# Gate and up weight gradients from one 512-column product, gate_w's gradient as one row, sines in one batch, the narrow products inside z

## The chip, the cores and the metric

The kernel runs on one core of a Trainium2 chip. The metric is the device time of one execution in microseconds (us). Five engines work side by side, each through its own queue in order: TensorE (PE in the profile; PEld are its weight loads), VectorE (DVE), ScalarE (ACT), GpSimd (POOL) and SyncE (SP), which here only issues DMAs. A matmul takes a stationary operand of up to 128 x 128 and streams the columns of a moving operand past it; its result goes to PSUM, from which ScalarE or VectorE copies it out ("evacuates" it) so that the PSUM buffer can be used again.

## The reference

The forward function mixes a spectral filter with a gated feed-forward network; the kernel computes its output and all gradients for a given `grad_out`. S = 2048 tokens, D = 576, F = 4608, all bf16.

```python
g = sigmoid((x * gate_w).sum(-1, keepdims=True))
a = irfft2(rfft2(x) * (w_r + 1j * w_i))                 # over tokens and features
b = (gelu(x @ w_gate) * (x @ w_up)) @ w_down
out = g * a + (1 - g) * b
# returned: out and the gradients of x, w_r, w_i, w_gate, w_up, w_down, gate_w
```

With da, the gradient at the hidden layer, the kernel needs A = gelu(.)*up, and the gradients dHg and dHu of the two hidden products; then dW_gate = x^T dHg, dW_up = x^T dHu and dW_down = A^T (grad_out (1 - g)).

## The kernel before

**First stage (up to 977 us).** The hidden width is cut into NG = 18 groups of FG = 256 columns. Each group takes four *steps* m = 0..3, one for each 512 tokens (four tiles of 128 tokens), so there are 72 steps `pr` = 4g + m. A step does on TensorE: 16 full matmuls of `z` (grad_out x w_down^T, L402, 256 columns) and 4 with 64 contraction rows (L407), 4 such ones of `xy` (L411, 512 columns: gate and up side by side), and two halves of 8 full ones (L418). ScalarE then reads z into `da` (L430) and each half of xy into `xb`, `hu` and `q` (L439, L440, L437). VectorE prepares the gelu (`H_ew1`, L445 to L447), ScalarE takes two sigmoids (L461, L462), and eight VectorE operations (`H_ew2`, L466 to L473) make A, dHu and dHg, which are kept in SBUF and also stored to a scratch tensor (L477).

**Weight gradients.** While group g runs, TensorE also does the products of group g - 1, which `W_units` hands out in portions to the four steps: `u_dwd` (dW_down: 4 units of 16 matmuls of 288 columns, L508), `u_dw` (dW_gate and dW_up over 512 of the 576 features: four units, each two PSUM halves of 16 matmuls with 256 columns, L527), and `tail` (the last 64 features: 16 pairs of matmuls with 64 stationary columns, L544). All share the PSUM pool `wps` of two buffers. A finished unit is evacuated by `wevac` (L486), on ScalarE as a rule, on VectorE while `wcopy[0]` says so, and stored from GpSimd's queue (L534, L518, L548).

**The spectral part.** Its 2-D transforms are a list of some 200 units of 2 to 12 matmuls (L574, L591, L683, L772, L818 and others). `want(pr)` says how many have to be done by step pr; `FIRST` lists this for the first eight steps. The first unit of a step goes between the matmuls of the second half of xy, the others between the portions of weight-gradient work ("jobs"), evenly by the jobs' estimated weights. All these units share a single PSUM buffer, which is also that of z: a unit can't begin before ScalarE has evacuated the one before it, and z of the next step not before the step's last one is out. An evacuation stands in ScalarE's queue where its unit was issued: that of the first unit before the reading of the second half of xy, that of the second one behind it.

**Tables.** The transforms need tables of sines. `build_R` and `build_B` compute angles on VectorE and put the sine itself on a list; `run_late` issues the listed sines on ScalarE (L170, L238), at steps 5 and 7. ScalarE needs another activation table for a sine than for a sigmoid. At steps 4 and 5, `scale_dB` multiplies grad_out by (1 - g), 16 tiles of 128 x 576, half on ScalarE (L956), half on VectorE (L958).

In group 0 the steps also hold the transposes of x and grad_out (`titems`, through two PSUM buffers `pg`) and the gate (`gate`, L383 to L387), which makes g.

**Second stage (from 977 us).** Every matmul has 288 columns (L1159): the output b, and the gradient of x. It ends with `x_last` for the last token tile. `gate_grad`, just before it, sums the gate's gradient over tokens by 10 matmuls (L1210) into a column of 576 numbers spread over the partitions, which GpSimd's queue stores by two DMAs with 2-byte elements (L1216, L1217). The last two stores of the x gradient are issued by SP (L1242).

```python
return [[d[0]], [d[1], d[2], d[3]], [tl_, w[0]], [w[1], w[2]], w[3]]   # L555: jobs of m = 0, 1, 2, 3; w[3] is carried to the next m = 0
FIRST = (0, 0, 0, 0, 0, 0, 3, 5)                                       # L921
tables = {5: 4, 7: 1}.get(pr)                                          # L1045: run_late before this job
```

Of the kernel before, what the change touches and what calls it, by code (L numbers as in the profile page):

```python
# [30 lines left out]
FG = 256  # L31
# [213 lines left out]
def kernel(  # L245
# [212 lines left out]
    def H_ew2(g, m, tiles, s, da):  # L458
        xb, q, hu = tiles
        om = ewt("om", g)  # L460
        nc.scalar.activation(om[:], s[:], ACT.Sigmoid, scale=-2.0 * C_GELU)  # L461
        nc.scalar.activation(s[:], s[:], ACT.Sigmoid, scale=2.0 * C_GELU)  # L462
        A = keepA.tile([P, 4, FG], BF16, tag="A", name="A")
        dHg = keep.tile([P, 4, FG], BF16, tag="dHg", name="dHg")
        dHu = keep.tile([P, 4, FG], BF16, tag="dHu", name="dHu")
        V.tensor_tensor(xb[:], xb[:], s[:], op=ALU.mult)  # L466
        V.tensor_tensor(q[:], xb[:], q[:], op=ALU.mult)
        V.tensor_tensor(om[:], om[:], q[:], op=ALU.mult)
        V.tensor_tensor(A[:], xb[:], hu[:], op=ALU.mult)
        V.tensor_tensor(dHu[:], da[:], xb[:], op=ALU.mult)  # L470
        V.tensor_tensor(om[:], om[:], s[:], op=ALU.add)
        V.tensor_tensor(hu[:], da[:], hu[:], op=ALU.mult)
        V.tensor_tensor(dHg[:], hu[:], om[:], op=ALU.mult)  # L473
        fsl = slice(g * FG, (g + 1) * FG)
        def store():
            for k, tl in enumerate((A, dHg, dHu)):
                LD.dma_start(scr[k][m][:, :, fsl].rearrange("t p f -> p t f"), tl[:])  # L477
        stores.append(store)
        kept.setdefault(g, []).append((A, dHg, dHu))
# [8 lines left out]
    def W_units(g):  # L488
# [3 lines left out]
        def tl(k, t):  # L492
            return kt[t // 4][k][:, t % 4, :]
# [27 lines left out]
        def u_dw(k, ov, c0, cut=T // 2):  # L521
            both = cut != T // 2

            def f(cc, t0, t1):
                wps = wtile(("w", k, c0))
                for t in range(t0, t1):
                    nc.tensor.matmul(wps[:, cc, :], lhsT=xn[:, t, (c0 + cc) * P:(c0 + cc + 1) * P],  # L527
                                     rhs=tl(k, t), start=(t == 0 and (cc == 0 or not both)),
                                     stop=(t == T - 1 and (cc == 1 or not both)))
                if cc == 0 or t1 < T:  # L530
                    return
                dw = stage.tile([P, TPB, FG], BF16, tag="dw", name="dw")
                wevac(dw[:], wps[:])
                wst[0].dma_start(ov[:, c0:c0 + TPB, fsl], dw[:])  # L534
            parts = [(cc, t0, t1) for cc in range(TPB) for t0, t1 in ((0, cut), (cut, T))]
            if both:
                parts.sort(key=lambda a: a[1])
            return [(1.7 * (a[2] - a[1]) / T, lambda a=a: f(*a)) for a in parts]
# [11 lines left out]
        tl_ = [(2.0, tail)]  # L550
        w = [u_dw(k, ov, c0, 12 if g == 0 and k == 1 else T // 2) for k, ov in ((1, o4v), (2, o5v)) for c0 in range(0, 4, TPB)]
        d = [u_dwd(fch, h) for fch in range(FCH) for h in range(2)]
        if g == 0:
            return [[w[0][:2], w[1][:2]], [w[0][2:], w[1][2:], tl_, d[0]], d[1:], [w[2]], w[3]]
        return [[d[0]], [d[1], d[2], d[3]], [tl_, w[0]], [w[1], w[2]], w[3]]  # L555
# [365 lines left out]
    FIRST = (0, 0, 0, 0, 0, 0, 3, 5)  # L921
# [31 lines left out]
    def scale_dB(n, on_act=False):  # L953
        for t in range(scaled[0], min(scaled[0] + n, T)):
            if on_act:
                nc.scalar.activation(dB[:, t, :], dB[:, t, :], ACT.Copy, scale=omg32[:, t:t + 1])  # L956
            else:
                V.tensor_scalar(dB[:, t, :], dB[:, t, :], omg32[:, t:t + 1], None, op0=ALU.mult)  # L958
            scaled[0] = t + 1

    for g in range(NG):
# [3 lines left out]
        for m in range(NPR):  # L965
# [3 lines left out]
            hs = [h for u in pend[m] for h in u] if pend else []  # L969

# [9 lines left out]
            if g == 0:  # L980
                def items(src, dst, t, *cp):
                    return titems(src, dst, 4 * t, (pgtile,) * 3, cp)
                head_, early, mid_, late_ = [
                    ([opening], [], items(dB, dOT, 1, VC, VC, VC) + items(xn, xT, 1, VC, VC, VC)
                     + [lambda: build_R(nc, tb, unit, 4)] + items(dB, dOT, 2, AC, AC, VC), []),
                    ([], items(xn, xT, 2, VC, VC, VC), [], items(dB, dOT, 3, AC, AC, VC)),
                    ([], items(xn, xT, 3, VC, VC, VC), [], []),
                    ([], [], [], [])][m]
                if m == 1:
                    rest.append(late_.pop())  # L990
                elif m == 2:
                    head_ = [rest.pop()]
                z, xy_full = H_mm(g, m, head_)
                da = H_da(g, m, z)
                for f in early:
                    f()
                if held:
                    held.pop()()
                xy = xy_full(0)
                for f in mid_:  # L1000
                    f()
                if m == 0:
                    columns_B(nc, tb, res)
                elif m == 1:
                    next(makeB)
                for part in (1, 0):
                    H_act(0, xy, tiles, part)
                xy = xy_full(1)
                for part in range(2):
                    H_act(1, xy, tiles, part)  # L1010
# [5 lines left out]
                for f in late_:  # L1016
                    f()
                state += [H_ew1(g, tiles), da]
                held.append(sigs)
            else:  # L1020
                z, xy_full = H_mm(g, m)
# [6 lines left out]
                xy = xy_full(1, fft_next if n else None)  # L1028
# [3 lines left out]
                if pr == 4:  # L1032
                    scale_dB(8, True)
                elif pr == 5:
                    scale_dB(8)
                elif pr == 6:
                    build_R(nc, tb, unit, 8)
                    next(makeB)
                elif pr == 7:
                    build_R(nc, tb, unit, 12)  # L1040
# [3 lines left out]
                at, k = 0.0, min(n, 1)  # L1044
                tables = {5: 4, 7: 1}.get(pr)  # L1045
# [64 lines left out]
    for _, h in carry + [h for us in pend[:4] for u in us for h in u] + pend[4]:  # L1110
        h()
    ps1.close()
# [10 lines left out]
    with tc.tile_pool(name="p2f", bufs=4, **kw) as p2f, \  # L1123
# [81 lines left out]
        def gate_grad():  # L1205
            gps = pacc.tile([P, 512], F32, tag="acc", name="gps")
            for c in range(5):
                n = min(P, D - c * P)
                for v in range(2):
                    nc.tensor.matmul(gps[0:n, c:c + 1], lhsT=gsplit[:, v, c * P:c * P + n], rhs=ones[:],  # L1210
                                     start=(v == 0), stop=(v == 1))
            dgw = p2s.tile([P, 5], BF16, tag="dgw", name="dgw")
            V.tensor_copy(dgw[:, 0:4], gps[:, 0:4])
            V.tensor_copy(dgw[LO, 4:5], gps[LO, 4:5])
            with nc.allow_non_contiguous_dma(reason="one column of 576 numbers"):
                ST.dma_start(out_7[0:512].rearrange("(c p) -> p c", p=P), dgw[:, 0:4])  # L1216
                ST.dma_start(out_7[512:D].rearrange("(p o) -> p o", o=1), dgw[LO, 4:5])  # L1217
# [96 lines left out]
```

## Time and profile before

| What | Value |
|---|---|
| Time, median of 3 runs | 1411.79 us (1410.51 to 1412.84) |
| The profiled execution's own time | 1411.65 us |
| Its span, first to last instruction | 1409.9 us |
| Mean granted TensorE clock | 0.996 |
| First stage / second stage | 0 to 977 us / 977 to 1409.9 us |
| VectorE, ScalarE busy over the span | 731.1 us, 738.6 us (52% each) |
| GpSimd busy | 225.4 us (16%) |
| DMA traffic | 214.62 MB, mean 152 GB/s |

A matmul's busy time overlaps that of its neighbours, so TensorE's busy share isn't how close it comes to its peak; the distance between the starts of matmuls is read from the timeline instead: n matmuls in a row that together last L, one of which lasts l, start (L - l)/(n - 1) apart. In the lists of waits each line gives who waited for whom, the total in us, how often, and the longest.

### The profile page before, as it was taken

How to read it: one execution, taken by the hardware profiler on the slowest of the kernel's cores; microseconds unless marked ns; L12 is line 12 of the kernel's file. 1: busy time of each engine (PE TensorE's matmuls, PEld its weight loads, DVE VectorE, ACT ScalarE, POOL GpSimd, SP SyncE). 2: the span in 40 equal slices, each digit the busy share in tenths (PEclk: the TensorE clock that was granted, in tenths of full speed). 3: DMA queues.
4: the chain of work that ended last, by engine and by line, in shares of the span. 5: the costliest groups of instructions: out<-in, count | busy, mean ns of one | idle time of the engine just before them, and what ended most of it. 6: DMA issues, size and time to landing. Idle time of an engine off the chain costs nothing.

```text
span 1409.9 us, 28154 instructions
## 1 busy us (share of the span) xinstructions
PE 1387.4 (98%) x11430; PEld 1027.5 (73%) x11430; DVE 731.1 (52%) x1393; ACT 738.6 (52%) x1334; POOL 225.4 (16%) x420
## 2 busy tenths in 40 slices
PE   8989999999999999999999999999999999999997
PEld 6566767676667766776776767778777777777776
DVE  7776565655788787785566565560001742122100
ACT  6877676777888888767777776661000000000000
POOL 3010100112343643322010100110000110000000
PEclk9999999999999999999999999999999999999999
DMA  6334344336455665555456465749999988777773
GB/s 206 102 85 134 94 137 119 110 113 167 124 152 138 165 162 153 138 144 150 139 147 169 123 170 155 168 111 277 192 195 201 231 188 169 161 158 165 156 150 70
DMA packets 509534, 214.62 MB, mean 152 GB/s; under 512 B 311418, under 2 KB 502588, under 8 KB 509404
## 3 DMA queue, kind: packets, MB, share of 16 engines
q1 hardware_dynamic: 493402, 187.44, 56.6%
q0 software_dynamic: 13872, 24.24, 6.0%
q8 instruction: 89, 1.46, 0.4%
q10 hardware_dynamic: 2130, 1.15, 0.3%
q14 instruction: 41, 0.34, 0.1%
HBM read 41.05 MB, written 93.84 MB: 96 GB/s over the span
## 4 chain that ended last, share of the span: by engine, by line
PE 94%; ACT 4%; DVE 1%; issue 0%; POOL 0%; POOLq 0%; DVEq 0%
PE acc L1159 30%; PE xy L418 17%; PE wps L527 17%; PE wps L508 10%; PE z L402 9%; PE wps L544 2%; PE xy L411 2%; PE pf L574 2%; PE z L407 2%; PE pf L844 1%; PE pf L772 1%; PE pf L591 1%; PE pf L846 1%; PE pf L818 1%; PE pf L683 1%; ACT q L437 0%
## 5 line engine op out<-in xcount | busy, mean ns | idle before, releaser
L1159 PEld LDWEIGHTS <-pin 128*128 128x128 bf16 x3456 | 338.0, 98 | 85.3 <-issue 0.2
L418 PE MATMUL xy<-wgu,xT 128*128 128x512 bf16 x1152 | 270.2, 380 | 0.0
L527 PEld LDWEIGHTS <-xn 128*128 128x128 bf16 x2304 | 223.9, 98 | 35.9 <-issue 1.0
L418 PEld LDWEIGHTS <-xT 128*128 128x128 bf16 x1152 | 106.5, 98 | 137.8 <-issue 29.5
L1176 ACT COPY bo<-acc 128x288 f32<-128x288 f32 x32 | 12.8, 400 | 304.5 <-PE acc L1159 304.5
L466 DVE TENSOR_TENSOR xb<-xb,s 128x1024 bf16<-128x1024 bf16 x72 | 49.9, 692 | 223.4 <-ACT s L462 223.2
L508 PE MATMUL wps<-dB,A 128*128 128x288 bf16 x1152 | 154.7, 287 | 0.0
L1159 PE MATMUL acc<-wgT,pin 128*128 128x288 bf16 x1152 | 143.8, 286 | 0.0
L1159 PE MATMUL acc<-wuT,pin 128*128 128x288 bf16 x1152 | 143.6, 286 | 0.0
L1159 PE MATMUL acc<-wd_all,pin 128*128 128x288 bf16 x1152 | 142.6, 286 | 0.0
L402 PE MATMUL z<-wdT,dOT 128*128 128x256 bf16 x1152 | 137.5, 273 | 2.4 <-ACT ve L594 1.6
L527 PE MATMUL wps<-dHg,xn 128*128 128x256 bf16 x1152 | 136.9, 273 | 0.0
L527 PE MATMUL wps<-dHu,xn 128*128 128x256 bf16 x1152 | 136.8, 272 | 0.0
L508 PEld LDWEIGHTS <-A 128*128 128x128 bf16 x1152 | 112.4, 98 | 31.7 <-issue 0.4
L402 PEld LDWEIGHTS <-dOT 128*128 128x128 bf16 x1152 | 112.5, 98 | 17.1 <-issue 2.9
L430 ACT ACTIVATE da<-z,omg 128x256 bf16<-128x256 f32 x288 | 112.2, 472 | 5.7 <-PE z L407 2.5
L534 POOL DMA_DIRECT2D out_dram<-dw x67 | 49.5, 738 | 399.1 <-ACT dw L486 375.9
L1236 DVE SCALAR_TENSOR_TENSOR f32t<-gwf,dlog,b16t 128x576 f32<-128x576 f32 x16 | 13.1, 817 | 172.3 <-DMA b16t<-dxa_scr 172.3
L439 ACT CAST xb<-xy 128x512 bf16<-128x512 f32 x144 | 85.6, 594 | 23.2 <-PE xy L418 23.2
L437 ACT ACTIVATE q<-xy 128x512 bf16<-128x512 f32 x144 | 88.2, 616 | 5.3 <-PE xy L418 1.5
L440 ACT CAST hu<-xy 128x512 bf16<-128x512 f32 x144 | 87.9, 610 | 0.0
L486 ACT CAST dw<-wps 128x512 bf16<-128x512 f32 x71 | 41.6, 589 | 83.4 <-PE wps L527 69.3
(214 smaller groups left out, 1709.4 us busy)
## 6 DMA issues: line engine op xcount, KB each, us to landing
scr<-A SPq DMA_DIRECT2D x72, 256.0 KB, 2.4
scr<-dHg SPq DMA_DIRECT2D x72, 256.0 KB, 3.1
scr<-dHu SPq DMA_DIRECT2D x72, 256.0 KB, 3.9
out_dram<-dw POOLq DMA_DIRECT2D x67, 128.0 KB, 2.8
wd_all<-in_B_w_down_dram SPq DMA_DIRECT2D x3, 1728.0 KB, 9.2
out_dram<-dwd POOLq DMA_DIRECT2D x34, 144.0 KB, 3.0
scr_p<-Vt SPq DMA_DIRECT2D x32, 145.0 KB, 3.0
wgu<-in_B_w_gate_dram SPq DMA_DIRECT2D x18, 256.0 KB, 4.1
```

Source lines behind the costliest of these rows:

```text
L402: nc.tensor.matmul(zo(t), lhsT=dOT[:, ci, t, :], rhs=wdT[:, ci, :], start=(t % 4 < 2 and ci == 0), stop=False)
L418: nc.tensor.matmul(xy[k][:, t % 2, :], lhsT=xT[:, ci, t, :], rhs=wgu[:, ci, :], start=False, stop=(ci == 3))
L430: nc.scalar.activation(da[:, t, :], z[:, t % 2, t // 2, :], ACT.Copy, scale=omg32[:, 4 * m + t:4 * m + t + 1])
L437: nc.scalar.activation(q[:, h, :], xy[:, :, 0:FG], ACT.Square)
L439: nc.scalar.copy(xb[:, h, :], xy[:, :, 0:FG])
L440: nc.scalar.copy(hu[:, h, :], xy[:, :, FG:2 * FG])
L466: V.tensor_tensor(xb[:], xb[:], s[:], op=ALU.mult)
L486: wcopy[0](out, in_)
L508: nc.tensor.matmul(wps[:, :288], lhsT=tl(0, t)[:, fch * P:(fch + 1) * P], rhs=dB[:, t, h * 288:(h + 1) * 288], start=(t == 0), stop=(t == ...
L527: nc.tensor.matmul(wps[:, cc, :], lhsT=xn[:, t, (c0 + cc) * P:(c0 + cc + 1) * P], rhs=tl(k, t), start=(t == 0 and (cc == 0 or not both)), ...
L534: wst[0].dma_start(ov[:, c0:c0 + TPB, fsl], dw[:])
L1159: nc.tensor.matmul(acc[:, :288], lhsT=src[:, r, :], rhs=w_of(r)[:, h * 288:(h + 1) * 288], start=(first and r == 0), stop=(last and r == F ...
```

## The change

Five edits:

1. dHg and dHu become the two halves of one tile `dH` of [128, 4, 2, 256], and `u_dw(c)` multiplies one chunk of 128 features with both at once: 16 matmuls of 512 columns in place of 32 of 256. A unit's result is stored by two DMAs of 128 x 256 in place of one of 128 x 512.
2. `tail` is no longer a job. It is issued inside `H_mm` at m = 2, between the full matmuls of z and its 64-row ones.
3. `gate_grad` turns operands round: a stationary column of ones, 288 moving columns, a row of 576 numbers in one partition, one DMA.
4. `run_late` runs once, at step 6; `build_R` and `build_B` move; `FIRST` starts the transforms later; `scale_dB` runs wholly on VectorE at step 4; in step 5 the rest of the first two `u_dw` units goes between the narrow and the full matmuls of xy, with their evacuation on VectorE.
5. In group 0 transposes move between the halves of xy.

```diff
@@ H_ew2
-        dHg = keep.tile([P, 4, FG], BF16, tag="dHg", name="dHg")
-        dHu = keep.tile([P, 4, FG], BF16, tag="dHu", name="dHu")
+        dH = keep.tile([P, 4, 2, FG], BF16, tag="dH", name="dH")
+        dHg, dHu = dH[:, :, 0, :], dH[:, :, 1, :]
...
@@ W_units
-        def u_dw(k, ov, c0, cut=T // 2):
...
+        def u_dw(c, cuts=(0, 4, 8, 12, T)):
+
+            def f(t0, t1):
+                wps = wtile(("w", c))
                 for t in range(t0, t1):
...
+                    nc.tensor.matmul(wps[:].rearrange("p a b -> p (a b)"), lhsT=xn[:, t, c * P:(c + 1) * P],
+                                     rhs=kt[t // 4][1][:, t % 4].rearrange("p k f -> p (k f)"), start=(t == 0), stop=(t == T - 1))
+                if t1 < T:
                     return
...
                 wevac(dw[:], wps[:])
-                wst[0].dma_start(ov[:, c0:c0 + TPB, fsl], dw[:])
...
+                for k, ov in enumerate((o4v, o5v)):
+                    wst[0].dma_start(ov[:, c, fsl], dw[:, k, :])
+            return [(3.45 * (b - a) / T, lambda a=a, b=b: f(a, b)) for a, b in zip(cuts, cuts[1:])]
...
-        tl_ = [(2.0, tail)]
-        w = [u_dw(k, ov, c0, 12 if g == 0 and k == 1 else T // 2) for k, ov in ((1, o4v), (2, o5v)) for c0 in range(0, 4, TPB)]
+        w = [u_dw(c, (0, 12, T)) if g == 0 and c < 2 else u_dw(c) for c in range(4)]
         d = [u_dwd(fch, h) for fch in range(FCH) for h in range(2)]
         if g == 0:
-            return [[w[0][:2], w[1][:2]], [w[0][2:], w[1][2:], tl_, d[0]], d[1:], [w[2]], w[3]]
-        return [[d[0]], [d[1], d[2], d[3]], [tl_, w[0]], [w[1], w[2]], w[3]]
+            return [[w[0][:1], w[1][:1]], [d[0], d[1]], [d[2], d[3]], [w[2], w[3][:2]], w[3][2:], {1: [w[0][1][1], w[1][1][1]], 2: [tail]}]
+        return [[d[0]], [d[1], d[2], d[3]], [w[0]], [w[1], w[2]], w[3], {2: [tail]}]
...
-    FIRST = (0, 0, 0, 0, 0, 0, 3, 5)
+    FIRST = (0, 0, 0, 0, 0, 0, 0, 2)
...
@@ the steps of group 0
-                z, xy_full = H_mm(g, m, head_)
+                do1 = items(dB, dOT, 1, VC, VC, VC) if m == 0 else []
+                do2 = items(dB, dOT, m + 2, AC, AC, VC)
+                x1 = items(xn, xT, m + 1, VC, VC, VC)
+                z, xy_full = H_mm(g, m, ([opening] if m == 0 else []) + rest)
...
+                if m == 0:
+                    early, mid_, late_ = do1[:2], [do1[2], x1[0]], x1[1:]
+                elif m < NPR - 1:
+                    early, mid_, late_ = x1[:2], x1[2:], []
...
+                if m + 2 < NPR:
+                    do2[0]()
+                    do2[1]()
+                    rest = [do2[2]]
...
@@ the other steps
-                z, xy_full = H_mm(g, m)
+                split = pr == 5
+                z, xy_full = H_mm(g, m, [] if split else inside)
+                if split:
+                    wcopy[0] = VC
+                    for f in inside:
+                        f()
+                    wcopy[0] = AC
                 xy = xy_full(0)
...
-                xy = xy_full(1, fft_next if n else None)
+                k0 = int(n > 0 and pr != 7)
+                xy = xy_full(1, fft_next if k0 else None)
...
                 if pr == 4:
-                    scale_dB(8, True)
+                    scale_dB(T)
                 elif pr == 5:
-                    scale_dB(8)
+                    build_R(nc, tb, unit, 8)
+                    build_R(nc, tb, unit, 12)
                 elif pr == 6:
-                    build_R(nc, tb, unit, 8)
                     next(makeB)
-                elif pr == 7:
-                    build_R(nc, tb, unit, 12)
...
-                tables = {5: 4, 7: 1}.get(pr)
+                tables = {6: 0}.get(pr)
...
@@ after the last step
     for _, h in carry + [h for us in pend[:4] for u in us for h in u] + pend[4]:
         h()
+    for f in pend[5][2]:
+        f()
...
@@ gate_grad
-            gps = pacc.tile([P, 512], F32, tag="acc", name="gps")
-            for c in range(5):
-                n = min(P, D - c * P)
+            dgw = p2s.tile([1, D], BF16, tag="dgw", name="dgw", bufs=1)
+            for h, ps in enumerate(acc_pair()):
+                hs = slice(h * 288, (h + 1) * 288)
                 for v in range(2):
-                    nc.tensor.matmul(gps[0:n, c:c + 1], lhsT=gsplit[:, v, c * P:c * P + n], rhs=ones[:],
-                                     start=(v == 0), stop=(v == 1))
...
+                    nc.tensor.matmul(ps[0:1, :288], lhsT=ones[:], rhs=gsplit[:, v, hs], start=(v == 0), stop=(v == 1))
+                V.tensor_copy(dgw[:, hs], ps[0:1, :288])
+            ST.dma_start(out_7.rearrange("(o d) -> o d", o=1), dgw[:])
```

## The prediction

> **What bounds the kernel now.** I read the page's busy shares, then its chain of waits, then the waits of TensorE and of SP, then timelines of the places they name.
>
> ```profile
> PE 1387.4 (98%) x11430; PEld 1027.5 (73%) x11430; DVE 731.1 (52%) x1393; ACT 738.6 (52%) x1334; POOL 225.4 (16%) x420
> PE 94%; ACT 4%; DVE 1%; issue 0%; POOL 0%; POOLq 0%; DVEq 0%
> ...
> PE wps L544 <- ACT dw L486: 4.1, 1, 4.1
> PE z L402 <- ACT ve L594: 1.6, 1, 1.6
> ...
> SPq L1309 <- DMA out_dram<-dgw: 5.2, 1, 5.2
> ```
>
> TensorE is the bound: only fewer columns, fewer pauses or an earlier end can help. Its two largest waits in the steps are 4.1 and 1.6 us. The third line is the end of the kernel: SP waits 5.2 us for the store of gate_w's gradient.
>
> How far the matmuls are from back to back, and what the first wait costs:
>
> ```profile
> 970.20 7.15 PE L527 MATMUL wps<-dHu,xn 128*128 128x256 bf16 x64
> 63.03 3.63 PE L418 MATMUL xy<-wgu,xT 128*128 128x512 bf16 x16
> 953.40 8.00 PE L508 MATMUL wps<-dB,A 128*128 128x288 bf16 x64
> 60.43 1.91 PE L402 MATMUL z<-wdT,dOT 128*128 128x256 bf16 x16
> 62.27 0.39 PE L407 MATMUL z<-wdT,dOT 64*128 64x256 bf16 x4
> 66.50:79.00 12.50, 8.37 (x67) 6.79 (x66) 9.20 (x20) 12.38 (x20) 2.83 (x4) 0.73 0.52 139
> ```
>
> (7.15 - 0.273)/63 = 109.2 ns for 256 columns; (3.63 - 0.379)/15 = 216.7 for 512; (8.00 - 0.286)/63 = 122.4 for 288. z to its 64-row part takes 1.84 us where 16 x 0.109 is 1.75: a change of shape costs 0.09. The last line sums the stretch 66.5 to 79 us, that of the 4.1 us wait: each engine's busy time, then the granted clock, 0.73 there and 1.00 in the stretches beside it. TensorE came back at half speed: from its return at 72.54 to the next z at 78.89 it did tail (16 pairs, 1.72 us at the later pace, and a change of shape) and 16 L508 (1.96) in 6.35 us instead of 3.77, so the wait cost another 2.6.
>
> **What the skill says.** "TensorEngine Tiling (Array Packing)", Key Properties: changing the tiling mode drains TensorE; the 0.09 us agree. "TensorE: Matmul & The Clock Gate", Part 1: an idle window of about 3.4 us halves the clock, a busy one restores it; the 0.73 agrees. "DMA: Bandwidth & Descriptors", Specifications: under 512 bytes a transfer becomes a read-modify-write; gate_w's two stores of 2-byte elements take 16.5 and 15.9 us to land, another store of 72 KB on the same queue 1.8. "VectorE: DVE Perf Modes", What auto-detection actually checks: the packed mode asks for 16-bit data with step 1. The halves of dH keep step 1, so I leave VectorE's 0.69 us as they are; the trace's strided stacks (L730, 578 elements, 457 ns) support it.
>
> **The parts.** *A, 512 columns.* 18 groups x 4 units x 16 = 1152 matmuls replace 2304; each saves 2 x 109.2 - 216.7 = 1.7 to 2.1 ns. **-2.2 us** (-2.8 to -1.5). The weight loads saved lie beside matmuls and bring nothing. The second store per unit costs GpSimd about 0.4 us (0.56 for 128 rows at L518, twice, against 0.74), hidden in its 84% idle time; the bytes and the 512-byte runs stay. After the last step ScalarE issues these stores, four more at 0.39, beside units of 3.5 us.
>
> *B, tail inside z.* Before: z to 64 rows, xy back to full, full to tail, tail to full, four changes at 0.09. After, z goes into tail, tail into 64 rows, xy back: three. No row shows tail next to 64 rows; I take the same 0.09. 17 x 0.09 = **-1.5 us** (-3.1 if that change is free, 0 if double). Tail now asks for its `wps` buffer earlier, that of the last dW_down unit but one, which was evacuated in the step before; behind tail stand the narrow matmuls and all of xy, so this cover is thick.
>
> *C, the end.* SP issues the last store at 1402.12, beside POOL's 1.8 us landing it is done at 1404.0; now SP is released at 1407.7, then waits 0.4 more for that store, which lands behind the small ones. Late next is the last store itself: 1408.4 - 1404.0 = **-4.3 us** (-4.8 to -3.3). Against it, four matmuls of 288 columns and two changes of shape (0.67) for ten tiny ones (0.43): +0.25.
>
> *D, the start.* Steps 0 to 3: the transposes between halves of xy remove waits of 0.5, but the second transposes of each pair still wait for the gate's sigmoid on ScalarE behind three reads of xy (0.8 us before), now twice. Walking the rows through, step 5 begins 0.4 earlier: -0.4.
> Step 5: the first W units are now evacuated on VectorE. Its queue holds ahead of them the gelu of step 3 (ends 62.2), `H_ew1` (1.5), all 16 scalings (16 x 0.29, from 2.32/8, = 4.6) and the eight operations of step 4 (5.2): 73.5, and the first copy ends at 74.2. TensorE reaches the dW_down unit that needs this buffer after z and narrow parts (2.6), 8 W matmuls (1.8) and 16 of xy (3.5): 60.0 + 7.9 = 67.9. It waits **6.3 us** in place of 4.1: the stall isn't removed, its cause moves from ScalarE's scalings (5.48 us) to VectorE's. With the clock halved for some 3.5 us after it (1.8 lost) it costs 8.1, against 4.3 + 2.6 before: +1.2.
> Steps 6 and 7: one pair of table loads (2 x 1.28 us) is saved on ScalarE, but the batch (1.28 + 4 x 0.64 + 0.47 + 1.28 = 5.6) still stands before the sigmoids and `da` of step 7, on which the first transform waits 1.1, the next 0.2; before, 1.7 at L402 and 0.24. Less 0.5. Sum of D **+0.3 us**. Below, -3: the idle stretch falls so that the clock stays full; above, +3.5: it stays halved for 3.4 us more, or VectorE's two strided writes a step lose the packed mode, which by their row would be some 0.5 us each in the chain from sigmoid through gelu to `da` of group 0.
>
> *E, the steps m = 2.* Tail was also the cover under which ScalarE read the second half of xy. Before, from a middle step (352 to 367):
>
> ```profile
> 359.67 1.02 PE L418 MATMUL xy<-wgu,xT 128*128 128x512 bf16 x4
> 362.50 0.42 PE L683 MATMUL pf<-Vp,Btab 128*128 128x289 bf16 x2
> 362.75 1.91 PE L527 MATMUL wps<-dHg,xn 128*128 128x256 bf16 x16
> 364.73 0.41 PE L683 MATMUL pf<-Vp,Btab 128*128 128x289 bf16 x2
> 366.72 1.80 PE L402 MATMUL z<-wdT,dOT 128*128 128x256 bf16 x15
> ...
> 360.21 1.29 ACT L688 CAST Xx<-pf 64x578 bf16<-64x578 f32 x2
> 361.52 0.60 ACT L437 ACTIVATE q<-xy 128x512 bf16<-128x512 f32 x1
> 363.39 1.28 ACT L688 CAST Xx<-pf 64x578 bf16<-64x578 f32 x2
> 365.17 1.29 ACT L688 CAST Xg<-pf 64x578 bf16<-64x578 f32 x2 [0.49 <-PE pf L683]
> ```
>
> The reader is to see that the second unit (362.50) comes 1.84 us of tail after xy ends, and the third one 1.98 later, each as its predecessor is out. In the changed program xy is followed by 4 matmuls of 512 (0.86), a unit, 8 (1.73), a unit, 4, next z. With xy's end as 0: the first evacuation ends at 1.10, so unit two waits 0.3, to 1.17, and is done at 1.4; ScalarE takes q, xb, hu (1.43) and starts its evacuation only at 2.56, to 3.84; unit three, due at 3.15, waits **0.76**, its evacuation runs 4.4 to 5.65, and z, due at 5.0, waits **0.7**. 1.8 us for three such units (two steps), 1.3 for two and one of L772 (evacuation 0.84; one step), 0.4 for three of L772 (two steps): 5.6, against 0.6 now: +5.0. The forward transforms have narrower evacuations (0.65) and longer units: walked likewise, 0.3 to 0.6 a step, as before. Inverse: 1.8 in four steps against some 1.1: +0.7. **E +5.7 us** (+2 to +11).
>
> *F.* The tables' transposes lose a wait of 0.7 at 313 us: -0.4. The drained tail is now last; VectorE's constants for the second stage overlie its staging buffer and come after its store (some 5.5 us to land at 978, as the row before it), about when TensorE asks for them: +0.4 (0 to 1).
>
> Sum: -2.2 - 1.5 - 4.3 + 0.25 + 0.3 + 5.7 - 0.4 + 0.4 = -1.75. The profiled execution took 1411.65, 0.14 under the median and 1.75 over its span of 1409.9; so 1411.79 - 1.75 = **1410.0 us**.
>
> **Rivals.** *R1, half the squeeze is hidden*: ScalarE gets through its reads earlier in m = 2 because z's part now runs longer. E is +2, the total -5.5: 1406.3. For it: ScalarE is idle during tail. Against: xy's second half can't be read before it is made. *R2, the first stall goes*: the copies are reached early on VectorE, or the clock isn't halved; D is -6 and the total -8: 1403.8. Against it: the order of the queue. *R3, slower*: the squeeze in m = 2 strikes all 14 steps with transforms, not mainly the five in the middle: at 0.85 us each E is 12, the total +4.5: 1416.3. It decides from E = 10.3, or 0.74 a step, where the sum passes +2.8. For it: a third of TensorE's work behind xy (1.8 of 5.3 us) has gone from there while ScalarE's is the same; against: the forward units come out at 0.3. That the stores of gate_w aren't the end (5.2 us are another DMA's) I hold at less than 5%, within the range.
>
> **How the numbers follow.** What a measurement of this kernel can tell from no change is about 0.2%, 2.8 us: faster is below 1409.0, slower above 1414.6. Forecast 0.48 (own range 1408.9 to 1413.5), R1 0.22, R2 0.12, R3 0.18. So faster 0.34, same 0.48, slower 0.18. The range leaves out R2's point and what of R3 lies above 1415.5: 1405.0 to 1415.5.
>
> **What would show it.** SP's wait for the row under 0.5 us, and the last store landing 2 us after its issue; L527 with 216 ns from start to start; TensorE waiting at L509 for VectorE's copy of step 5, with a granted clock under 1 after it; in middle steps m = 2 waits of 0.7 us before the third unit and before z. It is wrong if the first stall is under 3 us, if E's waits are absent or stand in every m = 2 step, or if the end moves by less than 3 us.

## The result and the profile after

The changed kernel takes 1422.38 us (median of 4 runs, 1421.6 to 1423.09) against 1411.15 for the kernel before on the same chip: the ratio is 1.0079, with a 95% interval of 1.0062 to 1.0097. It is 0.8% slower where no change was forecast, and 7 us above the forecast range. The profiled execution took 1423.09 us, with a span of 1421.3; before's span was 1409.9, so 11.4 us have to be found.

The list of what TensorE waited for, of the changed kernel (total, times, longest):

```profile
PE acc L1167 <- ACT dwt L486: 6.2, 1, 6.2
PE wps L509 <- DVE dw L486: 6.1, 1, 6.1
PE pf L768 <- DVE qn L738: 4.2, 2, 3.8
...
PE pf L768 <- DVE qm L738: 1.2, 1, 1.2
...
PE pf L679 <- ACT Xx L684: 0.8, 1, 0.8
PE pf L679 <- ACT Xg L684: 0.7, 1, 0.7
...
PE z L402 <- ACT Xx L684: 0.5, 1, 0.5
PE z L402 <- ACT Xg L684: 0.5, 1, 0.5
```

Before, the two largest were 4.1 and 1.6 us. The second line was forecast (6.3 us), and so were the last four. The first, the third and the fourth were not.

To see where the time went, take the start of each step in both traces (the first matmul of L402) and subtract. The difference, after minus before, grows like this:

| Stretch | Difference in it, us |
|---|---|
| up to the start of step 24 (where both have done all the units ahead of the middle transforms) | -0.5 |
| steps 24 to 45, the middle transforms | +9.7 |
| step 46 to the start of the second stage | -0.7 |
| second stage, to its last matmul | +8.1 |
| after the last matmul | -5.25 |
| **Sum** | **+11.4** |

In the middle, steps 28 and 29 alone lost 5.6 us, and 26, 30 and 38 lost 1.4, 1.6 and 1.4. In the second stage all is lost in its first 20 us. Between the stages ScalarE issues the stores of the last dW units, and SP issues three loads of w_down, 1.7 MB each. The timeline of ScalarE there, of the kernel before and then of the changed kernel (start, duration, operation; in brackets the idle time before it and what ended it; ACTq lines are issues of DMAs):

```profile
970.40 0.59 ACT L486 CAST dw<-wps 128x512 bf16<-128x512 f32 x1 [2.91 <-DMA out_dram<-dw]
971.80 0.39 ACTq L534 DMA_DIRECT2D out_dram<-dw  x1
973.89 0.59 ACT L486 CAST dw<-wps 128x512 bf16<-128x512 f32 x1 [2.91 <-PE wps L527]
976.97 0.38 ACTq L534 DMA_DIRECT2D out_dram<-dw  x1
977.92 0.59 ACT L486 CAST dw<-wps 128x512 bf16<-128x512 f32 x1 [3.44 <-DMA out_dram<-dw]
```

```profile
980.52 0.59 ACT L486 CAST dw<-wps 128x512 bf16<-128x512 f32 x1 [2.87 <-PE wps L527]
987.34 0.84 ACTq L534 DMA_DIRECT2D out_dram<-dw  x2
988.30 0.58 ACT L486 CAST dw<-wps 128x512 bf16<-128x512 f32 x1 [7.20 <-issue]
988.92 0.84 ACTq L534 DMA_DIRECT2D out_dram<-dw  x2
993.19 0.37 ACT L486 CAST dwt<-wps 128x256 bf16<-128x256 f32 x1 [4.30 <-DMA out_dram<-dw]
```

In the changed kernel a copy ends at 981.11, and its pair of stores is recorded at 987.34, 6.2 us later; the next copy stands behind it in ScalarE's queue ("issue": this view names no wait for it), and tail's copy behind that. What the store waited for, and what came after it, is in the profile's chain of waits, each step followed back to what released it:

```profile
976.91 10.36 DMA wd_all<-in_B_w_down_dram
987.27 0.02 issue
987.29 0.02 ACTq L534
987.30 0.04 issue
987.34 0.34 ACTq L534
987.68 0.04 issue
987.72 5.37 DMA out_dram<-dw
...
993.19 0.38 ACT dwt L486
```

The first load of w_down lands at 987.27, and ScalarE's store comes out right after it. The record at 987.29 is a wait: in the trace's instruction records the store reports its landing on the same semaphore (106) as that load, and it waits until the load is done with it. Tail's copy then waits 4.3 us more, for the second store of this pair to land: dw and dwt share a staging tile with two buffers (L336, L531, L543). A third buffer would have let tail's copy follow the issues that end at 989.76, an estimated 3.4 us earlier; no run tried it.

TensorE began the second stage at 985.74, needed the bank of tail's result after 12 matmuls, at 987.2, and got it at 993.6. Before, the same kind of delay was there (the copy of 973.89 ends at 974.48, its store comes at 976.97, 0.08 us after the first load of w_down has landed), but the last copy was done at 978.51 and the second bank was asked for at about that time (977.19 + 12 x 0.122 = 978.7): there was no margin, and nothing showed.

The windows (us; busy time and count of PE, PEld, DVE, ACT, POOL; the granted clock; DMA share; GB/s) show what the wait cost beyond itself:

```profile
987.00:994.00 7.00, 0.77 (x6) 0.42 (x4) 0.00 (x0) 0.96 (x2) 0.00 (x0) 0.70 1.09 362
994.00:999.00 5.00, 5.00 (x32) 3.48 (x30) 0.67 (x3) 0.00 (x0) 0.00 (x0) 0.73 0.43 124
```

After its return TensorE ran at a lowered clock: 32 matmuls in the second window, where 41 would fit at 122.4 ns, so another 1.1 us. With the wait this is most of the 8.1.

Step 28 of the changed kernel, on TensorE's timeline and then on VectorE's:

```profile
388.75 0.41 PE L768 MATMUL pf<-qm,BTtab 128*128 128x290 bf16 x2
389.00 1.89 PE L527 MATMUL wps<-dH,xn 128*128 128x512 bf16 x8
394.71 0.42 PE L768 MATMUL pf<-qn,BTtab 128*128 128x290 bf16 x2 [3.82 <-DVE qn L738]
394.97 3.10 PE L509 MATMUL wps<-dB,A 128*128 128x288 bf16 x16
```

```profile
376.61 1.43 DVE L704 TENSOR_TENSOR m<-Xx,Wt 128x1156 bf16<-128x1156 bf16 x2
...
390.24 1.43 DVE L704 TENSOR_TENSOR n<-Xg,Wt 128x1156 bf16<-128x1156 bf16 x2
391.76 1.87 DVE L726 TENSOR_TENSOR sn<-n,n 64x578 bf16<-64x578 bf16 x4
393.72 0.84 DVE L737 TENSOR_TENSOR qn<-sn 128x576 bf16<-128x576 bf16 x2
```

The unit needs qn, the folded product of the second transform chain. VectorE makes the m products in step 27 and the n products in step 28, just ahead of their use. Before, they were made a step earlier:

```profile
363.70 1.43 DVE L708 TENSOR_TENSOR m<-Xx,Wt 128x1156 bf16<-128x1156 bf16 x2
...
376.26 1.43 DVE L708 TENSOR_TENSOR n<-Xg,Wt 128x1156 bf16<-128x1156 bf16 x2
...
379.69 0.84 DVE L741 TENSOR_TENSOR qn<-sn 128x576 bf16<-128x576 bf16 x2
```

qn was then ready at 380.6 us, and its first unit ran at 388.32. The last forward unit of this group of transforms had come in step 25, at 352.0 us; in the changed kernel it comes in step 26, at 362.3. The 16 matmuls after the wait take 3.10 us instead of 2.12: the lowered clock again.

The end went the forecast way. SP's wait for a DMA in the last stretch, of the changed kernel:

```profile
SPq L1312 <- DMA out_dram<-b16t: 0.7, 1, 0.7
```

The wait of 5.2 us for gate_w's store is gone; the row lands 2.0 us after its issue.

### The profile page after: what moved, and what is told of

Read it like the earlier page. It is cut to its first block, busy times and chain, and to the rows that moved or that the text cites. A ratio compares the mean times of both kernels' runs of the same rounds, so it can differ in the third digit from the quotient of the medians.

```text
span 1421.3 us, 25906 instructions
## 1 busy us (share of the span) xinstructions
PE 1388.5 (98%) x10272; PEld 916.4 (64%) x10272; DVE 734.5 (52%) x1402; ACT 728.0 (51%) x1323; POOL 245.0 (17%) x486
## 4 chain that ended last, share of the span: by engine, by line
PE 65%; ACT 2%; DMA 1%; SPq 1%; DVE 0%; issue 0%; ACTq 0%; DVEq 0%
PE acc L1167 30%; PE xy L418 10%; PE wps L527 9%; PE wps L509 5%; PE z L402 5%; PE wps L541 1%; PE xy L411 1%; PE z L407 1%; SPq L1095 1%; DMA wd_all<-in_B_w_down_dram 1%; PE pf L840 1%; PE pf L842 1%; PE pf L768 1%; ACT ZT L817 0%; PE pf L814 0%; DMA out_dram<-dw 0%
## 5 line engine op out<-in xcount | busy, mean ns | idle before, releaser
L527 PE MATMUL wps<-dH,xn 128*128 128x512 bf16 x1152 | 270.9, 379 | 0.0
L418 PE MATMUL xy<-wgu,xT 128*128 128x512 bf16 x1152 | 270.4, 380 | 0.0
L418 PEld LDWEIGHTS <-xT 128*128 128x128 bf16 x1152 | 106.4, 98 | 136.6 <-issue 28.7
L527 PEld LDWEIGHTS <-xn 128*128 128x128 bf16 x1152 | 111.6, 98 | 118.7 <-issue 0.4
L534 POOL DMA_DIRECT2D out_dram<-dw x134 | 72.8, 547 | 447.2 <-ACT dw L486 366.5
L402 PE MATMUL z<-wdT,dOT 128*128 128x256 bf16 x1152 | 138.2, 273 | 2.2 <-ACT wdT L374 0.5
L402 PEld LDWEIGHTS <-dOT 128*128 128x128 bf16 x1152 | 112.9, 98 | 25.5 <-issue 5.0
L461 ACT ACTIVATE om<-s 128x1024 bf16<-128x1024 bf16 x72 | 76.3, 1060 | 5.8 <-DVE s L446 5.8
```

The costliest lines, as they stand in the source:

```text
L402: nc.tensor.matmul(zo(t), lhsT=dOT[:, ci, t, :], rhs=wdT[:, ci, :], start=(t % 4 < 2 and ci == 0), stop=False)
L418: nc.tensor.matmul(xy[k][:, t % 2, :], lhsT=xT[:, ci, t, :], rhs=wgu[:, ci, :], start=False, stop=(ci == 3))
L527: nc.tensor.matmul(wps[:].rearrange("p a b -> p (a b)"), lhsT=xn[:, t, c * P:(c + 1) * P], rhs=kt[t // 4][1][:, t % 4].rearrange("p k f -> ...
L534: wst[0].dma_start(ov[:, c, fsl], dw[:, k, :])
```

## The experiments

All times are compared with runs of the kernel before on the same chip. The changed kernel stands at 1.0079 on this scale, so a ratio of 1.0029, for instance, is 0.5% or 7 us faster than it; the intervals, about 0.0013 on each side for a run and 0.0017 for the changed kernel, make such a difference good to some 3 us.

### Between the stages: order, queue, loads, number of stores

**Tail ahead of the last four units.**

```diff
-    for _, h in carry + [h for us in pend[:4] for u in us for h in u] + pend[4]:
+    for _, h in carry + [h for us in pend[:2] for u in us for h in u]:
         h()
     for f in pend[5][2]:
         f()
+    for _, h in [h for us in pend[2:4] for u in us for h in u] + pend[4]:
+        h()
```

> The changed kernel, with the last group's tail unit put back ahead of the last four dW units in the part between the stages, nothing else. Theory: tail's place as the very last unit costs 8 us, since its copy stands behind the dW copies on ScalarE, these behind their stores, and the second stage's second output bank behind tail's copy; so 7 to 8 us faster than the changed kernel (1414.5 to 1415.5 us), no wait over 1.5 us at the start of the second stage. Rival: the stores of this stretch are late whatever the order (two per unit where there was one, beside three loads of w_down), and the last dW copy holds the second stage instead: less than 3 us faster, and the wait is there with dw in place of dwt.

1422.74 us against 1412.97, ratio 1.0073 (1.0060 to 1.0086): 0.8 us less than the changed kernel. The rival holds: the place of tail isn't the cause. A store of this run comes out at 987.17, after the first load has landed at 987.15, and TensorE's list names another copy, with nearly the same wait:

```profile
PE acc L1169 <- ACT dw L486: 5.9, 1, 5.9
```

**GpSimd issues the stores.**

```diff
-    wst[0] = nc.scalar
```

> The changed kernel, with the stores between the stages issued by GpSimd, as all before them are, in place of ScalarE; order of the units unchanged. If the wait of 6.2 us at the second stage's start comes from ScalarE standing in its own queue before it can issue a store (one is issued at 987.3 us, for a copy that ended at 981.1), the copy of tail comes right after its matmuls and the wait falls under 1.5 us: 5.5 to 7.5 us faster. If it comes from the DMA engines being full (their share reads 1.1 in this stretch), so that the stores land no earlier whoever issues them, the time stays within 2 us of the changed kernel.

1416.80 us against 1412.97, ratio 1.0029 (1.0018 to 1.0040): 7 us less than the changed kernel. The copies of ScalarE come earlier, and TensorE's wait is 0.5 us:

```profile
985.72 0.59 ACT L486 CAST dw<-wps 128x512 bf16<-128x512 f32 x1 [4.62 <-DMA out_dram<-dw]
987.40 0.37 ACT L486 CAST dwt<-wps 128x256 bf16<-128x256 f32 x1 [1.09 <-DMA out_dram<-dw]
```

The 4.62 us for an earlier store to land show that the transfers are slow here whoever issues them. That delay alone cost TensorE 0.5 us; what cost the 7 us was the store that waited for a load. In the traces GpSimd's DMAs report on eight semaphores of their own (111 to 118), which no load of SP uses.

**The loads of w_down later.**

```diff
-    for f0 in range(0, NFC, FCB):
-        LD.dma_start(wd_all[:, f0:f0 + FCB, :], wd_v[:, f0:f0 + FCB, :])
...
                 used[0] += 1
                 ensure()
+                if t == 0 and k == 1:
+                    LD.dma_start(wd_all[:, f0:f0 + FCB, :], wd_v[:, f0:f0 + FCB, :])
```

> The changed kernel, with the three loads of w_down (1.7 MB each) issued one by one during the second stage's first job in place of ahead of it. Theory: these loads are what ScalarE's store stands behind (SP issues them from 976.9 to 985.4 us, ScalarE's third pair of stores comes out at 987.3, 6.3 us after its copy). Without them the copies end as the matmuls do and the 6.2 us wait falls under 1.5: 5 to 8 us faster, if the loads still land before the fourth job asks for them, some 26 us into the stage. Rival: ScalarE's stores wait for one another, or for the transposing loads of the second stage: less than 2 us faster.

1425.09 us against 1413.45, ratio 1.0083 (1.0069 to 1.0096): no gain. But the wait has moved. Without the loads ScalarE's stores follow their copies at once (981.59 + 0.59, then 982.21), TensorE takes up the second stage without a pause, and at 1013.9 us it waits for a transposed operand instead, whose loads were now issued in turn with those of w_down. ScalarE's timeline, then a line of TensorE's list:

```profile
981.59 0.59 ACT L486 CAST dw<-wps 128x512 bf16<-128x512 f32 x1 [2.87 <-PE wps L527]
982.21 0.82 ACTq L534 DMA_DIRECT2D out_dram<-dw  x2
```

```profile
PE acc L1165 <- DMA pin<-scr: 5.9, 1, 5.9
```

So what held the stores were the loads of w_down on SP's queue, as the chain has it; as a remedy, moving them only trades one wait for another.

**The kernel before, with two stores per unit.**

```diff
-                wst[0].dma_start(ov[:, c0:c0 + TPB, fsl], dw[:])
+                for j in range(TPB):
+                    wst[0].dma_start(ov[:, c0 + j, fsl], dw[:, j])
```

> The kernel before, with each dW unit's 128 KB store split into two of 64 KB, as the change has them; nothing else of the change. Theory: between the stages two stores per unit on ScalarE's queue fall behind the loads of w_down that SP issues there, the copies stand behind them, and the second stage waits for a bank, as in the changed kernel in either order: 4 to 8 us slower than before, with a wait on ScalarE's dw at the start of the second stage. Rival: the number of stores doesn't matter, only where the units and the loads fall in time: within 1.5 us of before.

1422.46 us against 1413.45, ratio 1.0066 (1.0053 to 1.0078): 9 us slower, the theory's case and 1 us beyond its range, by one edit that moves no byte more. Its profile has the wait at the same place:

```profile
PE acc L1160 <- ACT dw L486: 5.3, 1, 5.3
```

The second stage of this trace is 7.3 us longer than before's; 3.3 more stand after the last matmul, where gate_w's old stores are, and are not accounted for. In the 72 steps, where GpSimd issues the stores, nothing is lost. The doubled number of stores is enough to bring on nearly the whole loss between the stages. Why the number counts can be read from the semaphores: with two stores per unit it is a store of the second of the last four units that reports on the first load's semaphore (its copy ends at 970.45, the store comes out at 976.57), and two more units stand behind it; in the kernel before it is the third unit's.

### The middle: lag of the units, products, tail

**The lag made up for.** `want` counts from 5 again, less a lag that goes from 3 at step 8 to 0 at step 16.

```diff
-        n0 = FIRST[-1]
+        n0 = 5
...
-        return int(min(n, n_slots) + 1e-9)
+        return int(min(n, n_slots) + 1e-9) - max(0, 3 - (pr - 7) // 3)
```

> The changed kernel, with the three transform units that steps 6 and 7 no longer hold made up for by step 16 (the count of units lags by 3, 2, 1, 0 of the kernel before's), so that from step 16 on every step holds the same number of units as before the change. Theory: the 4.0 us wait before the third unit of step 28 and the 1.4 us of step 30 come from this lag: the products on VectorE are started by the last forward unit of a group, which now falls one step later, and the next unit that needs them doesn't. Then both waits go, steps 28 to 30 lose 5 to 6.5 us and the whole is 4.5 to 6.5 us faster; the 0.9 and 0.7 us in steps 26 and 38 stay. Rival: these are the same squeeze as in steps 26 and 38, tail's missing time: less than 1.5 us faster.

1418.42 us against 1412.97, ratio 1.0040 (1.0027 to 1.0054): 5.5 us less than the changed kernel by the ratios, 3.0 by the two spans: at the start of step 24, by when both have done the same units, this one is 2.6 us later, and why is not shown. Steps 28, 29 and 30 are 4.9, 0.7 and 0.9 us shorter, no wait for qn or qm of 0.2 us or more is left in the list, and those of steps 26 and 38 stay.

**More products in step 27.**

```diff
-                side_work(4.4)
+                side_work(9.0 if pr == 27 else 4.4)
```

> The changed kernel, with VectorE's budget for products in step 27 raised from 4.4 to 9.0, nothing else. Theory: the 3.8 us wait in step 28 is the second product chain (n), which step 27 has no budget for, since the first one (m) reaches it a step later than before; with it in step 27 that wait goes, and the whole is 3 to 4.5 us faster. Rival: VectorE is full in step 27, and what is added there makes the gelu chain late: within 1.5 us of the changed kernel.

1421.15 us against 1413.16, ratio 1.0056 (1.0043 to 1.0068): 3.2 us less. Both sides were partly right. Step 28 loses its wait (it is 4.9 us shorter), but step 27 gets one of 3.3 us, before a forward unit whose predecessor ScalarE hadn't evacuated, and is 3.5 us longer; steps 29 to 31 give another 1.8.

**Tail behind xy again.**

```diff
-        return [[d[0]], [d[1], d[2], d[3]], [w[0]], [w[1], w[2]], w[3], {2: [tail]}]
+        return [[d[0]], [d[1], d[2], d[3]], [[(2.0, tail)], w[0]], [w[1], w[2]], w[3], {}]
```

> The changed kernel, with tail of every group put back behind the second half of xy in the steps m = 2 (and so ahead of the last four dW units between the stages, which alone was worth 1.4 us). Theory: tail's place inside z takes the cover from ScalarE's reads of xy. Back behind xy, the waits of 0.9 and 0.7 us in steps 26 and 38 go (1.3 each), the 1.4 in step 30 shrinks, and 1.5 us of shape changes return: 2 to 4.5 us faster than the changed kernel; the 3.8 us of step 28 stay. Rival: these waits come from the lag of the units too: then this is 0 to 1.5 us slower than the run with tail first between the stages.

1418.84 us against 1413.45, ratio 1.0039 (1.0026 to 1.0053): 5.6 us less by the ratios, 2.9 by the two spans (step 0, which the edit doesn't touch, is 1.7 us longer in this one). Step by step: 26 and 38 each 1.39 us shorter, 29 and 30 together 1.95, step 28 0.7 longer. That the waits of steps 26 and 38 were tail's missing cover is shown: they went with tail's return, while the run that made up the lag kept them.

### The start: the two copies of step 5

```diff
-                    wcopy[0] = VC
                     for f in inside:
                         f()
-                    wcopy[0] = AC
```

> The changed kernel, with the copies of the first two dW units in step 5 made by ScalarE, as elsewhere, in place of VectorE. Theory: TensorE's 6.1 us wait in step 5 is VectorE's queue (16 scalings and a gelu chain ahead of the copies). ScalarE reaches them after its sigmoids at about 65.4 us and is done at 66.6, before TensorE asks at 67.6: the wait goes, and with it the half clock after it. Step 5 becomes 7 to 8 us shorter, of which up to 3 come back in steps 6 to 8, where VectorE is then late: 4 to 8 us faster. Rival: the scalings themselves hold TensorE (its dW_down unit reads the scaled rows), and the wait stays at 2 us or more with dB named: under 3 us faster.

1416.23 us against 1412.97, ratio 1.0026 (1.0019 to 1.0033; single runs from 1414.37 to 1419.59): 7.5 us less than the changed kernel. Step 5 is 8.5 us shorter, and TensorE no longer waits in it. Step 7 gives 1.3 back: its first unit waits 2.2 us instead of 0.9 for da, which ScalarE makes after the batch of sines.

### The end: the row by itself

The kernel before, with the `gate_grad` of the diff and nothing else.

> The kernel before with gate_w's gradient stored as one row, nothing else of the change. In the profile of the changed kernel the stretch after the last matmul is 5.25 us shorter than before. Theory: that is the row's, and adds up with the rest, so 4.0 to 5.3 us faster than the kernel before. Rival: the end depends on when the second stage begins and on which transfers are still under way, and alone the row is worth less than 2.5.

1405.94 us against 1413.16, ratio 0.9951 (0.9939 to 0.9964): 7 us faster than before, above the expectation. The profiled execution, the slowest of the five at 1407.27, is 4.4 us shorter in span than before's: what follows the last matmul is 4.95 us shorter (8.28 us there, then 3.33), the second stage 0.5 longer. The other 2 to 3 us aren't explained; the granted clock reads 0.999 in the other four runs, and 0.995 to 0.997 in the runs of before, which only locates them on TensorE.

### Three mends, then five

The edits of GpSimd's stores, the lag and the two copies together:

> The changed kernel with three mends together: GpSimd's stores between the stages (7.3 us alone), the units made up for by step 16 (5.7), the two dW copies of step 5 on ScalarE (7.9). If the three are apart, the sum is 21 us off the changed kernel: 1402 to 1405 us, 8 to 10 us under the kernel before. If they cover one another in part (the copies on ScalarE press the same steps as the earlier units), it is 1406 to 1410.

1407.68 us against 1413.45, ratio 0.9963 (0.9950 to 0.9975): faster than before, but 3 to 4 us short of the sum by the ratios, 2.1 by the spans. The place of 1.6 of these is step 7: 16.7 us long, against 13.9 in the changed kernel and 15.2 with the copies alone. ScalarE still makes the sines there, and VectorE the last of their angles, while TensorE is some 8 us ahead of where it was.

Two more edits on top:

```diff
-    FIRST = (0, 0, 0, 0, 0, 0, 0, 2)
+    FIRST = (0, 0, 0, 0, 0, 0, 0, 0)
...
-        return int(min(n, n_slots) + 1e-9) - max(0, 3 - (pr - 7) // 3)
+        return int(min(n, n_slots) + 1e-9) - max(0, 5 - (pr - 7) // 3)
...
+        if 5 <= g <= 9:
+            return [[d[0]], [d[1], d[2], d[3]], [[(2.0, tail)], w[0]], [w[1], w[2]], w[3], {}]
         return [[d[0]], [d[1], d[2], d[3]], [w[0]], [w[1], w[2]], w[3], {2: [tail]}]
```

> The run with three mends, and two more: no transform unit in step 7 (the count lags by 5 units from step 8 and is made up for by step 22), and tail behind the second half of xy again in m = 2 for the groups whose units run in steps 26 to 42. Theory: in the run with three mends step 7 took 16.7 us because its first unit waited 2.2 us for the sigmoids and da behind the batch of sines, and the clock halved after it; with no unit there step 7 loses 3 to 4.5 us beyond the moved units (each some 1.1 us, given back in later steps). Tail brings 1.3 each in steps 26 and 38 and up to 1 in step 30. Together 4 to 8 us off the run with three mends: 1400 to 1404 us. Rival: the wait for da moves to the next user of ScalarE or VectorE in step 7 or 8 and only tail's 2 to 3.5 remain: 1404 to 1406.

1401.28 us against 1413.16, ratio 0.9919 (0.9906 to 0.9933): 0.8% faster than the kernel before, as the theory had it. Step 7 is 5.5 us shorter than with three mends, steps 26 and 38 1.4 each, 30 and 34 0.7 and 0.6. TensorE's list begins with 46 gaps of 0.2 us at L418, where 68 matmul records are missing from this trace; then follow:

```profile
PE pf L367 <- ACT g_bf L385: 2.4, 3, 1.0
PE pf L865 <- POOL ident masks.py:199: 1.4, 1, 1.4
PE pf L842 <- ACT ZT L819: 1.4, 2, 1.1
```

No wait above 1.4 us is left in it, and the mean granted clock is 1.000.

## Why the prediction was wrong, step by step

**A, 512 columns.** Right, a little small. The changed kernel's unit of dW, from TensorE's timeline:

```profile
969.96 13.98 PE L527 MATMUL wps<-dH,xn 128*128 128x512 bf16 x64
```

(13.98 - 0.379)/63 = 215.9 ns, so each matmul saves 2 x 109.2 - 215.9 = 2.5 ns: 2.9 us in all where 2.2 were taken; 2.8 was the end of its range. VectorE's writes into the halves of dH took 0.69 us, as before. But the step failed in its last sentence, and this is the first step of the prediction that failed: "After the last step ScalarE issues these stores, four more at 0.39, beside units of 3.5 us." The stores were priced at their issue, as if a queue that is 0.39 us busy were free; the wait ahead of the issue was put at nothing. In that stretch SP issues three loads of 1.7 MB, and a ScalarE store waited 6.2 us for the first of them to land; the second stage lost 8.1 us. This is the largest error, and it was in plain sight: before's timeline has two stores there that come 0.8 and 2.5 us after their copies.

**B, tail inside z.** Three changes of shape as forecast; z to tail costs 0.093, tail to 64 rows 0.095, as assumed for the unseen pair. The 1.5 us stand.

**C, the end.** 5.25 us in the trace after the last matmul, against 4.3 (3.3 to 4.8). Right in mechanism, a little small; by itself the edit was worth 7 us in the medians, of which 2 to 3 aren't explained.

**D, the start.** The wait in step 5 is 6.1 us (6.3 forecast), and copying on ScalarE instead brings 7.5 us, against the 8.1 at which wait and clock were priced. At step 24, -0.5 is left; with five groups of A and B (-0.8, -0.45) and the wait before the tables' transposes (0.5 in before's list, not 0.7) taken out, D comes to about +1.2 in place of +0.3.

**E, the steps m = 2.** The walk through the rows was good: +4.7 us for the five middle steps, 5.3 with A's and B's share in them taken out (5.0 forecast), with the waits at the forecast places in 26 and 38. Part of this fit is luck: step 30 lost 1.6 us, and 0.9 of it went when the lag of the units was made up for, which the walk didn't have. The step failed, as the second of the prediction, because it walked only the steps where tail had stood, and took every operand of a unit as ready. `FIRST` was counted as an edit of steps 6 and 7; that `want` spreads the three units over the whole list, so that the middle steps are still one or two behind, was not followed. That put the last forward unit of a group from step 25 into 26, VectorE's two product chains a step later, and 5.6 us into steps 28 and 29. The inverse transforms fit their +0.7: steps 46 to the end of the stage come to -0.7 with 1.7 us of A and B in them, so to about +1.0, with one middle unit more than before.

**F, between the stages.** "VectorE's constants ... +0.4" looked at the right moment and the wrong engine; TensorE waited for ScalarE's copy, and it was +8.1. In the list of chances the slower outcome stood at 0.18, for the squeeze in all 14 steps; that mechanism isn't what happened. By its own list of what would make it wrong, none was met: the first stall was there, E's waits stood where they should, the end moved by more than 3 us. The losses came from two places that the list did not name.

Taken by the measured terms: -0.5 to step 24, +4.7 and +5.6 in the middle with -0.6 in its other steps, -0.7, +8.1, -5.25 make the 11.4 us of the two spans.

The clock step was sound in size. "TensorE: Matmul & The Clock Gate" in the Trainium skill, Part 1, gives an idle window of about 3.4 us for halving; waits of 3.8, 6.1 and 6.2 us were each followed by a lowered clock (0.69, 0.62 and 0.73 in the windows after them).

## What to carry to other kernels

Before pricing a DMA at its issue time, look at what else is being issued in that stretch, and at how long after its copy the store is recorded in the timeline: the gap shows a wait, the chain names what ended it, and an evacuation behind a held store holds a PSUM bank. When a schedule is counted by quota, shift the quota by one and ask for each consumer whether its producer moved too. A wait that has no margin in the trace of before (a copy that ends just as its bank is asked for) can be a cost that the next edit pays.

## What the runs showed of the hardware

- Stores issued by ScalarE were held up to 6.2 us beside SP's large loads; the same stores from GpSimd were issued at 0.5 us each, right after their copies (7 us less in all). The hold lies in the program's semaphores. In all traces here the DMAs of SP and of ScalarE report their landing on the same eight semaphores, and one that gets a semaphore still in use waits until the DMA that has it has landed. In all nine runs in which ScalarE stores beside these loads, the held store comes out 0.02 to 0.08 us after the first load's landing, which takes 9.2 to 10.7 us from its issue. Splitting a 128 KB store in two was enough to bring this on (9 us). "DMA: Bandwidth & Descriptors" in the Trainium skill says under "Issuing engines are not separate DMA queues" that using several engines for issuing saves only the sequencer's time, "which is usually small relative to the DMA itself". The issue itself fits that (0.34 us); the 7 us came from the semaphores, which depend on the issuing engine in these programs.
- A pause of 2.2 us was once followed by a lowered clock and once not. With three mends and with the copies alone, step 7 pauses alike, in front of the same unit; the windows after it, of the former and then of the latter:

```profile
91.80:97.00 5.20, 5.20 (x20) 2.38 (x20) 5.06 (x9) 3.37 (x7) 0.00 (x0) 0.67 0.25 74
```

```profile
91.80:97.00 5.20, 5.20 (x29) 2.62 (x28) 4.58 (x9) 3.98 (x9) 0.00 (x0) 1.00 0.35 105
```

The granted clock is 0.67 in one and 1.00 in the other, and step 7 takes 16.7 and 15.2 us: 1.5 us by the clock. So a wait well below the 3.4 us named above can cost more than its length; why it did so in one run only is not shown. It may be part of the 5 us between the single runs with the copies alone, which is not shown either.
